# One weight block ahead of an activation tile, and a small early read of the other weight blocks

## The chip, the cores and the metric

The kernel runs on one core of a Trainium2 chip. TensorE (PE) multiplies, VectorE (DVE), ScalarE (ACT) and GpSimd (POOL) do the elementwise work, SyncE (SP) and ScalarE issue DMA transfers, which run on the core's 16 DMA engines. The metric is the device time of the whole program in microseconds (us).

## The reference

A linear-attention block and a dense GELU block share one layer-normalized input, and both are added to it:

```
xn = _layernorm(A_x)                       # A_x: 1 x 2048 x 640, bf16
# A: 32 heads of 20
q, k, v = split(xn @ wqkv)
phi(t) = where(t > 0, t + 1, exp(t)) + 1e-6
kv  = einsum("bhsd,bhse->bhde", phi(k), v);  z = einsum("bhsd->bhd", phi(k))
o   = einsum("bhqd,bhde->bhqe", phi(q), kv) / (einsum("bhqd,bhd->bhq", phi(q), z) + 1e-6)
A   = o @ wo
# B: F = 1536
B   = gelu(xn @ w1 + b1) @ w2 + b2
out = A_x + A + B
```

## The kernel before

Tokens are cut into 16 tiles of 128 (x0 to x15), the width 640 into 5 blocks of 128 (DT = 5), the hidden width 1536 into 12 blocks (JT = 12). W1 is loaded in five row blocks of 128 x 1536, one for each block of the contraction; each is 384 KB, a token tile of x is 160 KB.

The program issues every engine's instructions in the order in which they are written. A small planner (class Planner) notes for each tile who wrote it and who reads it, and gives an instruction the semaphore waits that follow; it doesn't reorder. Each DMA has a semaphore of its own, which sixteen increments complete.

The kernel has these stages: the hidden layer (xn @ w1, GELU) for all tokens while x, W1 and then the other weights arrive; the key features (L556 on); two products over tokens; the query features with the small products between; and the output, which sums over HG (the hidden layer) and PQ (the query features).

The change touches the first microseconds. SP issues, in order (L268 to L277): x0, x1, W1's row blocks 0 to 3 (`dma_w1`, L266), x2, W1's block 4, x3, and then x4 to x11 in three DMAs. ScalarE issues one early load, b1 (L449), after the warming activation at L448.

Meanwhile PE runs nine products on zeros (L318, L452; the last six open the accumulation in six banks). Tile 0 is normalized: statistics on DVE (`ln_half`, L331) with a small addition on POOL (L334), aggregation and reciprocal on DVE (L339, L342), a square root on ACT (L343), and three partial normalizations on DVE (`norm_part`, L398). PE transposes the pieces (`transp_part`, L404) and ACT copies them back (`copy_part`, L415). Tile 1 follows on the same engines, but takes its inverse root by a power on POOL (L346), and its first copy is on DVE (L413).

The hidden layer of tiles 0 and 1 is made block by block of the contraction, so that it can begin when W1's first block is there. `pass_k(k, t, n, ...)` (L421, matmuls at L424) multiplies W1's row block k for all twelve hidden blocks with n tiles from t on. PE's queue has, from the first of these on: pass 0 of tile 0 (four matmuls), the last transposes of tile 0, the other eight of pass 0, pass 1, **the five transposes of tile 1**, pass 2 of tile 0, the transpose of b1 (L323), passes 0 to 2 of tile 1, and passes 3 and 4 for both tiles at once, with the GELUs on ACT (L432). Tiles 2 and 3 follow (`h_two`, L439) and then wider units (`h_unit`, L380).

The buffer kT (two buffers of 128 x 512) is used by the key features: `phi` writes it (L562) and a DMA transposes it from there (L563). Nothing writes it before.

Of the kernel before, what the change touches and what calls it, by code (L numbers as in the profile page):

```python
# [7 lines left out]
P = 128  # L8
# [104 lines left out]
def bass_parallel_sum__linear_attn_block__dense_activation_gelu__prompt_kernel(  # L113
# [8 lines left out]
    DT = D // P  # L122
# [15 lines left out]
    with contextlib.ExitStack() as es:  # L138
# [41 lines left out]
        kT = sb("kT", [P, 2, CW], BF16)  # L180
# [55 lines left out]
        r_kT = [R_("kT%d" % i) for i in range(2)]  # L236
# [19 lines left out]
        def dma_x(t, n):  # L256
            src = xv[t * P:(t + n) * P, :].rearrange("(t p) d -> p t d", p=P)
            Pl.ins("sync", lambda e: e.dma_start(x_in[:, t:t + n, :], src),  # L258
                   writes=r_x[t:t + n], dma=True)

        def dma_w(eng, dst, src, res):
            Pl.ins(eng, lambda e: e.dma_start(dst, src), writes=[res], dma=True)

        w1v = B_w1.rearrange("(k p) n -> p k n", p=P)
        wqv = A_wqkv.rearrange("(k p) n -> p k n", p=P)
        def dma_w1(k):  # L266
            dma_w("sync", W1[:, k, :], w1v[:, k, :], r_W1[k])
        dma_x(0, 1)  # L268
        dma_x(1, 1)
        for k in range(4):  # L270
            dma_w1(k)
        dma_x(2, 1)
        dma_w1(4)
# [42 lines left out]
        def filler(n):  # L316
            b = take(1)
            Pl.ins("tensor", [lambda e: e.matmul(bank(b), warm[:, 0:P], warm[:], start=True, stop=True)  # L318
                              for _ in range(n)], reads=[r_warm], writes=[B_[b]])
# [126 lines left out]
                    reads=[B_[b], r_b1c], writes=[r_HG[t][jb + a]])  # L446

        Pl.ins("scalar", lambda e: e.activation(b1c[:, 0:1], warm[:, 0:1], ACT.Sqrt), reads=[r_warm], writes=[r_b1c])  # L448
        dma_w("scalar", b1tmp[:], B_b1.rearrange("(a p) -> a p", p=P), r_b1tmp)  # L449
        filler(3)  # L450
        for i in range(NB):
# [419 lines left out]
```

## Time and profile before

| | |
|---|---|
| median of 3 runs | 205.04 us (204.85 to 205.44) |
| the profiled execution | 204.63 us |
| its span (first to last instruction) | 203.2 us |
| PE busy | 198.3 us (98% of the span) |
| DVE, ACT, POOL busy | 122.2, 73.5, 13.7 us |
| granted TensorE clock | 1.0 |
| x0, x1, W1 block 0: issue to landing | 2.2, 2.2 and 4.4 us |

In the profile, rows of instructions have line, engine, operation, the tile written and the tile read, the shapes, a count, and the time. PEld is the weight load of TensorE. "Idle before" is the time that the engine waited just ahead, with what ended it in brackets. A W1 row block appears as "W" read from in_B_w_dram. The chain that ended last is followed back from the last instruction to what released each; its rows are start, length and what. Matmuls are pipelined, so a row's length runs to a modelled end, and neighbouring starts tell the pace.

### The profile page before, as it was taken

Reading aid. Unit: us, or ns where it says so; the run is one execution under the profiler, and the core shown is the slowest. Engines: PE = TensorE matmul, PEld = TensorE weight load, DVE = VectorE, ACT = ScalarE, POOL = GpSimd, SP = SyncE. Lnnn points to the kernel's source line nnn. Section 1 sums busy time; section 2 is a strip of 40 time slices with the busy share of each in tenths; the row PEclk is TensorE's granted clock in tenths of the full one; section 3 lists DMA queues with packets and bytes.
Section 4 is the critical chain, followed back from the end, with each engine's and each line's share of the span. In section 5 each row is a group of like instructions: output and inputs, shape, how many; then the busy total and the mean of one; then the engine's idle time right before and its main releaser. Section 6 shows DMA issues by size and latency. Waiting matters only on the chain.

```text
span 203.2 us, 3231 instructions
## 1 busy us (share of the span) xinstructions
PE 198.3 (98%) x1178; PEld 106.9 (53%) x1195; DVE 122.2 (60%) x246; ACT 73.5 (36%) x148; POOL 13.7 (7%) x41
## 2 busy tenths in 40 slices
PE   6899999999999999999999999999999999999996
PEld 2799984444444444644456565444444444444444
DVE  3669873000005899999458899693893685356222
ACT  3469996666667555111233596200000000000000
POOL 1135444000000000000000000000000000000000
DMA  6964898899901111000269935119276727633521
GB/s 164 391 224 97 135 203 112 269 320 267 277 0 26 26 26 29 0 0 0 41 185 374 147 65 105 48 36 161 39 104 198 147 45 150 165 76 64 168 77 52
DMA packets 51285, 25.45 MB, mean 125 GB/s; under 512 B 38134, under 2 KB 50630, under 8 KB 51270
## 3 DMA queue, kind: packets, MB, share of 16 engines
q1 hardware_dynamic: 47790, 24.07, 49.2%
q10 hardware_dynamic: 3480, 1.18, 2.5%
q8 instruction: 9, 0.15, 0.3%
q14 instruction: 6, 0.05, 0.1%
HBM read 12.72 MB, written 2.62 MB: 76 GB/s over the span
## 4 chain that ended last, share of the span: by engine, by line
PE 96%; DMA 2%; issue 1%; SPq 0%; DVE 0%
PE ps L780 29%; PE ps L380 19%; PE ps L619 11%; PE ps L608 8%; PE ps L567 8%; PE ps L745 7%; PE ps L424 3%; PE ps L439 3%; DMA W<-in_B_w_dram 2%; PE ps L598 2%; PE ps L558 2%; PE ps L633 1%; PE ps L651 1%; SPq L258 0%; PE ps L404 0%
## 5 line engine op out<-in xcount | busy, mean ns | idle before, releaser
L780 PE MATMUL ps<-HG,W 128*128 128x512 bf16 x188 | 41.9, 379 | 0.2
L380 PE MATMUL ps<-xnT,W 128*128 128x512 bf16 (+1 forms) x222 | 39.0, 336 | 0.2
L380 PEld LDWEIGHTS ps<-xnT,W 128*128 128x128 bf16 x225 | 22.0, 98 | 16.7
L780 PEld LDWEIGHTS ps<-HG,W 128*128 128x128 bf16 x192 | 18.8, 98 | 22.6
L384 ACT ACTIVATE HG<-ps,b1c 128x512 bf16<-128x512 f32 (+1 forms) x45 | 26.3, 667 | 11.3 <-PE ps L380 10.8
L619 PE MATMUL ps<-xnT,Wqkv 128*128 128x512 bf16 x97 | 22.4, 380 | 0.2
L567 PE MATMUL ps<-Wqkv,xnT 128*128 128x512 bf16 x78 | 17.8, 379 | 0.1
L780 PE MATMUL ps<-PQ,Msb 128*128 128x512 bf16 x78 | 17.8, 379 | 0.1
L608 PE MATMUL ps<-xPK,xn_tm 128*128 128x512 bf16 x78 | 17.2, 379 | 0.1
L331 DVE BATCH_NORM_STATS2 stats<-xPK 128x6 f32<-128x320 bf16 x32 | 13.8, 470 | 4.3 <-DMA xPK<-in_A_x_dram 4.3
L619 PEld LDWEIGHTS ps<-xnT,Wqkv 128*128 128x128 bf16 x100 | 11.3, 118 | 8.7
L542 ACT ACTIVATE xn_tm<-ps 128x512 bf16<-128x512 f32 x20 | 11.9, 597 | 9.5 <-PE ps L619 8.9
L786 DVE SCALAR_TENSOR_TENSOR W<-ps,b2c,xnT 128x512 bf16<-128x512 f32 x16 | 11.6, 738 | 5.9 <-PE ps L780 5.5
L545 DVE SCALAR_TENSOR_TENSOR PQ<-ps,xn_tm 128x512 bf16<-128x512 f32 x20 | 13.8, 692 | 2.1
L542 ACT ACTIVATE ek<-ps 128x512 bf16<-128x512 f32 x20 | 11.8, 597 | 8.4 <-PE ps L567 6.4
L553 DVE CAST b2c<-out_l 128x5 f32<-128x5 bf16 x1 | 0.2, 172 | 22.4 <-DMA out_l<-b2bc 22.4
L567 PEld LDWEIGHTS ps<-Wqkv,xnT 128*128 128x128 bf16 x80 | 7.8, 98 | 9.4
L780 PEld LDWEIGHTS ps<-PQ,Msb 128*128 128x128 bf16 x80 | 7.8, 98 | 9.4
L608 PEld LDWEIGHTS ps<-xPK,xn_tm 128*128 128x128 bf16 x80 | 7.8, 98 | 9.3
L668 DVE SCALAR_TENSOR_TENSOR xn_tm<-PQ,z_sb,xn_tm 128x512 f32<-128x512 bf16 x16 | 12.0, 750 | 0.4
L684 DVE TENSOR_REDUCE den_sb<-xn_tm 128x128 f32<-128x512 f32 x4 | 4.2, 1040 | 13.4 <-DMA xn_tm<-xn_tm 13.4
L545 DVE SCALAR_TENSOR_TENSOR xPK<-ps,ek 128x512 bf16<-128x512 f32 x16 | 11.1, 692 | 1.7
(73 smaller groups left out, 182.2 us busy)
## 6 DMA issues: line engine op xcount, KB each, us to landing
xPK<-in_A_x_dram SPq DMA_DIRECT2D x5, 640.0 KB, 8.1
Wqkv<-in_A_wqkv_dram SPq DMA_DIRECT2D x3, 800.0 KB, 6.8
W<-in_B_w_dram SPq DMA_DIRECT2D x5, 384.0 KB, 5.4
W<-in_B_w_dram SPq DMA_DIRECT2D x1, 1920.0 KB, 14.8
out_dram<-xPK SPq DMA_DIRECT2D x3, 640.0 KB, 3.5
xPK<-in_A_x_dram SPq DMA_DIRECT2D x4, 320.0 KB, 5.3
xn_tm<-xn_tm ACTq DMA_DIRECT2D x12, 64.0 KB, 3.2
Wo<-in_A_wo_dram SPq DMA_DIRECT2D x1, 750.0 KB, 11.5
```

Of the source, the lines that this page charges most:

```text
L331: Pl.ins(v, lambda e: e.bn_stats(stats[:, s, 6 * h:6 * h + 6], x_in[:, t, h * HW:(h + 1) * HW]), reads=[r_x[t]], writes=[r_stats[s][h]])
L380: Pl.ins("tensor", [(lambda e, k=k: e.matmul(bank(b, 0, w), W1[:, k, jb * P:(jb + 1) * P], xnT[:, k, tok], start=(k == 0), stop=(k == DT - ...
L384: Pl.ins("scalar", lambda e: e.activation(HG[:, jb, tok], bank(b, 0, w), ACT.Gelu_apprx_tanh, bias=b1c[:, jb:jb + 1]), reads=[B_[b], r_b1c ...
L542: Pl.ins("scalar", lambda e: e.activation(et, src, ACT.Exp), reads=[B_[b]], writes=[re])
L545: Pl.ins(v, lambda e: e.scalar_tensor_tensor(out=dst, in0=src, scalar=0.0, in1=et, op0=ALU.max, op1=ALU.add), reads=[B_[b], re], writes=[r ...
L567: Pl.ins("tensor", [(lambda e, k=k, b=b, t=t: e.matmul(bank(b), xnT[:, k, t * P:(t + 1) * P], Wqkv[:, k, D:D + CW], start=(k == 0), stop=( ...
L608: Pl.ins("tensor", lambda e, t=t, b=b, f=f: e.matmul(bank(b), xn_tm[:, t, f * P:(f + 1) * P], PK[:, t, 0:CW], start=(t == 0), stop=(t == N ...
L619: Pl.ins("tensor", [(lambda e, k=k, j=j, b=b: e.matmul(bank(b), Wqkv[:, k, j:D:DT], xnT[:, k, cc], start=(k == 0), stop=(k == DT - 1))) fo ...
L668: Pl.ins(v, lambda e: e.scalar_tensor_tensor(out=yv[c % 2], in0=pq, scalar=z_sb[:, j:j + 1], in1=yv[c % 2], op0=ALU.mult, op1=ALU.add), re ...
L745: return lambda e: e.matmul(bank(b, 0, cs.stop - cs.start), l, r[:, cs], start=(i == 0), stop=(i == JT + DT - 1))
L780: Pl.ins("tensor", lambda e, l=l, r=r, i=i: e.matmul(bank(b), l, r, start=(i == 0), stop=(i == JT + DT - 1)), reads=rd, writes=[B_[b]], ma ...
L786: Pl.ins(v, lambda e: e.scalar_tensor_tensor(out=oT[o], in0=bank(b), scalar=b2c[:, nb:nb + 1], in1=xnT[:, nb, cc], op0=ALU.add, op1=ALU.ad ...
```

## The change

SP now issues x0, W1's block 0, x1, and then W1's blocks 1 to 3; the rest keeps its order. ScalarE issues one more DMA ahead of b1's: it reads 32 elements (64 bytes) of the first 16 rows of each of W1's row blocks 1 to 4 and writes them into the first buffer of kT, on 16 partitions. What it writes is never read; the planner registers it as a writer of that buffer. Nothing else is different (line numbers after it move by one or two).

```diff
@@ -266,8 +266,9 @@
         def dma_w1(k):
             dma_w("sync", W1[:, k, :], w1v[:, k, :], r_W1[k])
         dma_x(0, 1)
+        dma_w1(0)
         dma_x(1, 1)
-        for k in range(4):
+        for k in range(1, 4):
             dma_w1(k)
         dma_x(2, 1)
         dma_w1(4)
@@ -446,6 +447,7 @@
                     reads=[B_[b], r_b1c], writes=[r_HG[t][jb + a]])
 
         Pl.ins("scalar", lambda e: e.activation(b1c[:, 0:1], warm[:, 0:1], ACT.Sqrt), reads=[r_warm], writes=[r_b1c])
+        dma_w("scalar", kT[0:16, 0, 0:P].rearrange("p (k n) -> p k n", k=4), w1v[0:16, 1:DT, 0:32], r_kT[0])
         dma_w("scalar", b1tmp[:], B_b1.rearrange("(a p) -> a p", p=P), r_b1tmp)
         filler(3)
         for i in range(NB):
```

## The prediction

> **What bounds the kernel now.** I read the busy shares first. PE is busy for nearly the whole span, at full granted clock, so time can only be won or lost where PE waits.
>
> ```profile
> span 203.2 us, 3231 instructions
> PE 198.3 (98%) x1178; PEld 106.9 (53%) x1195; DVE 122.2 (60%) x246; ACT 73.5 (36%) x148; POOL 13.7 (7%) x41
> ```
>
> Then the chain that ended last, in order of time, for the first 16 us. The reader is to see that it enters PE at 6.17 through the load of W1's first row block, and that from 8.40 on it is PE work with no wait.
>
> ```profile
> 1.73 4.40 DMA W<-in_B_w_dram
> 6.13 0.05 issue
> 6.17 0.40 PE ps L424 x4
> 6.57 0.11 PE ps L404 x2
> 6.68 0.45 PE ps L424 x8
> 7.13 0.02 issue
> 7.15 0.84 PE ps L424 x12
> 8.00 0.41 PE ps L404 x5
> 8.40 0.67 PE ps L424 x12
> ```
>
> This chain would promise up to half a microsecond: the first product of pass 0 also needs a copy (L415) that ends at 5.59, so with W1's block 0 there PE could start near 5.65 instead of 6.17. But the five transposes at 8.00 (L404, token tile 1) stand in PE's queue ahead of pass 2, and they wait for something else. So third I read VectorE's timeline.
>
> ```profile
> 4.68 0.82 DVE L398 TENSOR_SCALAR xn_tm<-xPK,aggr,rstd 128x128 bf16<-128x128 bf16 x3 [0.27 <-ACT rstd L343]
> 5.42 0.88 DVE L331 BATCH_NORM_STATS2 stats<-xPK 128x6 f32<-128x320 bf16 x2
> 6.40 0.21 DVE L339 BATCH_NORM_AGGREGATE aggr<-stats 128x2 f32<-128x12 f32 x1
> 7.37 0.64 DVE L398 TENSOR_SCALAR xn_tm<-xPK,aggr,rstd 128x256 bf16<-128x256 bf16 x2 [0.76 <-POOL rstd L346]
> ```
>
> The statistics of x1 start at 5.42 with no idle time ahead of them: DVE has just finished tile 0. Statistics, aggregation, GpSimd's power (6.69 to 7.26) and the two normalizations follow without a gap that anything else fills. The second normalization ends at 8.00, and the single matmul records show the third transpose starting at 8.06. The two before it start at 7.83 and 7.89; at the 0.056 us between neighbours the third would have come at 7.94 had it waited for W1 alone. So at 8.06 two chains meet, the W1 side ready at 7.94 and the x1 side at 8.06, and **the x1 side already ends last**. From the start of x1's statistics to that transpose are 8.06 - 5.42 = 2.64 us.
>
> Last, the landings. A DMA counts sixteen engines and is complete with the last. Asked issue by issue, the DMA view gives 2.2 us from issue to landing for x0 and for x1, and 4.4 for W1's block 0. In the trace's records of the increments x0 is complete at 2.98, x1 at 3.58, block 0 at 6.13, block 1 at 7.11, block 2 at 8.05. Block 0's sixteen increments are thirteen from 4.84 to 5.07, then 5.22, 5.69 and 6.13. Why so late shows in the stretches of the DMA traffic (columns: stretch, length, busy of PE, PEld, DVE, ACT, POOL, clock, DMA share, GB/s):
>
> ```profile
> 2.80:3.20 0.40, 0.40 (x2) 0.15 (x1) 0.20 (x1) 0.00 (x0) 0.00 (x0) 1.00 1.48 360
> 3.20:3.60 0.40, 0.40 (x2) 0.15 (x1) 0.40 (x2) 0.00 (x0) 0.02 (x1) 1.00 0.82 92
> 3.60:4.00 0.40, 0.40 (x2) 0.15 (x1) 0.29 (x2) 0.00 (x0) 0.21 (x1) 1.00 0.67 200
> 4.00:4.80 0.80, 0.77 (x3) 0.10 (x1) 0.49 (x3) 0.20 (x1) 0.00 (x0) 1.00 1.08 346
> ```
>
> From 3.2 to 4.0 the engines move little. In the packet records a W1 packet (3072 B) takes 0.121 us, but the first ones of block 0 take 0.35 to 0.84, and one, at 3.91, takes 1.14. Block 1's first packets, at 4.4 to 4.7, take 0.12 to 0.62; x packets (1280 B) take 0.055, the first ones of x0 and x1 up to 0.39. [...] the slowest engine carries it along: it stays some 0.45 us behind the second slowest from block 0 to block 3.
>
> [...] b1's packets, ScalarE's one early load, lie at 2.30 to 2.79 among x0's and x1's. [...]
>
> **The change part by part.**
>
> (1) W1's block 0 is issued before x1. SP's issues are 0.47 apart (0.80, 1.27, 1.73), so block 0 is issued at 1.27 and x1 at 1.73; all later SP issues keep place and time, and the engines have a backlog anyway. Per engine block 0 is 8 packets, 8 x 0.121 = 0.97 us, and x1 is 8 x 0.055 = 0.44. Block 0 no longer has x1's 0.44 ahead of it: it is complete near 6.13 - 0.44 = 5.7, and PE starts at about 5.7, 0.45 earlier. Pass 1 still waits for block 1, which has the same bytes ahead as before (7.11), so the W1 side stays at 7.94. This saves nothing at 8.06.
>
> x1 now is the last of the first three transfers. The bytes of x0, x1 and block 0 together are what they were, so if the stalls stay, x1 is complete when block 0 was: 6.13. VectorE is free for it at 5.42. The statistics start at 6.13 + 0.03 = 6.16, 0.74 later, and all behind them on DVE (aggregation, normalization, the copy L413) and POOL shift likewise; the third transpose starts at 6.16 + 2.64 = 8.80. PE, done with pass 1 near 7.9, idles. Pass 2 is late by 0.74, and so is everything after, since from 8.40 on the chain has no other wait that could absorb it (x2, 9.43, has about 1 us of slack in front of it on DVE). Cost: +0.74. If x1's engines are all as quick as the fifteenth was (5.69) it is 5.72 - 5.42 = +0.30; if as the thirteenth (5.07), nothing. So x1 costs nothing when complete by 5.39 and one for one after that.
>
> (2) The small read: one more DMA issue on ScalarE ahead of b1's. The only such row is b1's issue, 0.63 us from 1.23; now the small one takes 1.23 to 1.86 and b1's follows to about 2.5. ScalarE's next work that matters is the square root at 4.44: hidden by 1.9 us; b1 itself is first used by a transpose at 9.0. The transfer is 64 packets of 64 bytes, four per engine, one in each block 1 to 4, arriving near 2.30 as b1's packets did. Moving them costs little: b1's 256 B packets took 0.018 us, so 4 x 0.018 = 0.07 per engine. What they may cost is first-read stalls, in front of block 0 and x1, and for engines not yet through with x0 (its packets run to about 2.6) in front of x0. The trace shows no such read. Below: none, as the stalls run beside the one that block 0's first packet has anyway (0.23 to 0.72 over the 0.121); an early read of W1 could even shorten block 0's long second stall (1.14 - 0.12 = 1.0), a gain for x1 of up to 0.74, after which DVE binds. Above: four stalls in a row of block 1's worst excess, 0.62 - 0.12 = 0.50 each, 2.0 us. I take 0: mostly beside block 0's own stall, with some delay against some relief. The stalls of blocks 1 to 4 that go away save nothing, as x1 binds.
>
> (3) The scratch is kT's first buffer, whose first true write is by DVE in the key phase, after 60 us: one more wait, long met. Nothing.
>
> Sum: 0 for W1 + 0.74 for x1 + 0 for the small read = +0.74, on the profiled execution 204.63 + 0.74 = 205.37 (span 203.2 + 0.74 = 203.9, and 1.4 around it as before). The profiled execution lies 0.41 below the median of the runs shown, 205.04; on that median it is 205.78, so 205.8.
>
> **The rivals.** Bounds first: I call 0.3% (0.62 us), about what a measurement of this kernel can tell from no change, the edge of "same".
>
> Rival A, not slower: x1 is complete by about 5.4 to 5.9 because the long stall doesn't come back, cured by the small read or mere bad luck of one engine. For it: thirteen of sixteen engines were done with block 0 by 5.07, and x1 would need only those. It decides at x1 complete at 5.39, and up to 5.39 + 0.62 = 6.01 it stays within "same". Time 205.0 to 205.6. Against: the last engine decides[...].
>
> Rival B, much slower: the small read's stalls come one after the other, or in front of x0's last packets, where each delays tile 0 as well and so everything one for one. +0.74 plus 0.5 to 2.0: 206.3 to 207.8. For it: b1's packets reach the engines at 2.30, when x0 isn't through. Against: x packets follow each other at 0.055 us although a whole DMA takes 2.2 from issue to landing, so reads overlap within an engine, and four stalls can too.
>
> Rival C, faster: W1's blocks stall longer in the timed runs than in the profiled one (the 0.41), and the small read removes that, while x1 comes in time. Then PE gains what it waits for W1 beyond 8.06: at most some 0.4 to 0.8, 204.2 to 204.6. Against: nothing of it shows in the profile, where the x1 side ends last.
>
> **How the numbers follow.** Forecast (x1 late by 0.6 to 1.2): 0.42; rival A 0.37; B 0.14; C 0.07. Forecast and B are slower by over 0.3%: 0.56. A is "same": 0.37. C is faster: 0.07. The predicted time is the forecast's, 205.8, its own range 205.6 to 206.3. The range for 8 in 10 leaves out most of C and the far end of B: 204.7 to 206.8.
>
> **What would show it.** Right: block 0 complete at 5.6 to 5.8 and PE's first L424 there; DVE's second pair of L331 with an idle time in front put down to x's DMA, starting at about 6.1; PE idle ahead of the tile 1 transposes, which end near 9.1 instead of 8.40; and the same shift, not more, at each later point of the chain. Wrong: if the second pair of L331 still starts at 5.42, the forecast falls for A; if the first pair starts after 3.00, the small read sits in front of x0 (B); if the chain's 8.40 comes earlier, then tile 1's transposes weren't bound by x1 as I read them.

## The result, and the profile after

The changed kernel took 206.77 us (median of 4 runs, 206.36 to 206.98), the kernel before 205.24 us beside it (204.85 to 205.45, 4 runs): a ratio of 1.0074, 95% interval 1.0051 to 1.0098. Later sets of the same two kernels, below, do not repeat that ratio. Of the later runs 18 were over 1.5% above the fastest of their kernel (17 of the kernel before, one of the small read alone) and are left out of the counts, group medians and means below.

The page of the kernel after, its span and busy time:

```profile
span 205.3 us, 3249 instructions
PE 199.6 (97%) x1195; PEld 106.9 (52%) x1195; DVE 122.5 (60%) x246; ACT 74.5 (36%) x148; POOL 13.7 (7%) x41
```

The span is 2.1 us longer. The chain that ended last (start, length, what) now enters PE through x1, not through W1:

```profile
1.73 4.10 DMA xPK<-in_A_x_dram
5.83 0.02 issue
5.85 0.90 DVE stats L332 x2
...
7.81 0.36 DVE xn_tm L399
8.16 0.05 issue
8.21 0.29 PE ps L405 x2
8.50 0.00 issue
8.50 0.34 PE ps L405 x3
8.84 0.67 PE ps L425 x12
```

x1 is complete at 5.83, its statistics start at 5.85 instead of 5.42, and pass 2 starts 0.44 later (8.84 for 8.40). PE's own timeline shows both sides of the swap: the first product starts 0.38 earlier than before (5.79 for 6.17) and waits for ACT's copy, no longer for W1, whose block 0 is complete at 4.77 instead of 6.13; and PE idles 0.54 ahead of tile 1's transposes, where it didn't before.

```profile
5.79 0.38 PE L425 MATMUL ps<-xnT,W 128*128 128x128 bf16 x4 [0.15 <-ACT xnT L416]
8.21 0.63 PE L405 MATMUL ps<-ident,xn_tm 128*128 128x128 bf16 x5 [0.54 <-DVE xn_tm L399]
```

So far this is the forecast with 0.44 in place of 0.74. Comparing the two traces weight load by weight load, the changed kernel is 0.43 late from tile 1's transposes on, and 2.07 late from the first weight load of L380 (L381 after the change) on, until the end. The second loss, 1.64, is one wait. The chain of the kernel before from 14 us on goes from tiles 2 and 3 (L439) to the wider units (L380) without a wait:

```profile
14.20 6.88 PE ps L439 x120
21.07 8.95 PE ps L380 x82
```

The chain of the kernel after between 14 and 30 us:

```profile
14.63 6.88 PE ps L440 x120
21.52 1.44 issue
22.96 7.15 PE ps L381 x64
```

At 21.52 PE has finished tiles 2 and 3 and stands until 22.96. "Issue" means that the profile names nothing that it waited for; what it needs there is tiles 4 and 5, whose transposes are DMAs (L506). In the DMA view of the issue of tile 5's transpose (count, time from issue to landing) the kernel after has

```profile
xnT<-xn_tm SPq DMA_TRANSPOSE x1, 4.3
```

against, in the kernel before,

```profile
xnT<-xn_tm SPq DMA_TRANSPOSE x1, 2.6
```

where it was issued at 18.09 and complete at 20.66, 0.19 ahead of PE's need at 20.85. In the kernel after it was issued at 18.52 and complete at 22.87. The DMA queues of the kernel after from 20.4 to 21.8 (queue, packets, MB, time as a share of 16 engines):

```profile
q1 hardware_dynamic: 456, 0.11, 122.9%
q8 instruction: 1, 0.02, 5.1%
```

The packet of the second row is a 16 KB fetch of instructions, at 20.50, 1.14 us long; in these two traces such fetches (0.88 to 1.41 us) recur every 78 to 164 weight loads of PE, counted at their ends. Here it begins as the transpose's last packets are due. In the kernel before the fetch of that place began at 21.78, after tile 5 and within tile 6's transpose, which then took 4.3 us (19.41 to 23.71) and was not yet needed.

### The profile page after: what moved, and what is told of

Read it like the earlier page. It is cut to its first block, busy times and chain, and to the rows that moved or that the text cites. A ratio compares the mean times of both kernels' runs of the same rounds, so it can differ in the third digit from the quotient of the medians.

```text
span 205.3 us, 3249 instructions
## 1 busy us (share of the span) xinstructions
PE 199.6 (97%) x1195; PEld 106.9 (52%) x1195; DVE 122.5 (60%) x246; ACT 74.5 (36%) x148; POOL 13.7 (7%) x41
## 4 chain that ended last, share of the span: by engine, by line
PE 94%; DMA 2%; issue 1%; DVE 1%; SPq 0%; POOL 0%; DVEq 0%
PE ps L782 29%; PE ps L381 19%; PE ps L621 11%; PE ps L569 8%; PE ps L610 8%; PE ps L747 7%; PE ps L440 3%; PE ps L425 3%; PE ps L600 2%; PE ps L560 2%; DMA xPK<-in_A_x_dram 2%; PE ps L635 1%; PE ps L653 1%; DVE stats L332 0%; PE ps L405 0%
## 5 line engine op out<-in xcount | busy, mean ns | idle before, releaser
L381 PE MATMUL ps<-xnT,W 128*128 128x512 bf16 (+1 forms) x225 | 39.1, 336 | 1.4 <-issue 1.4
L385 ACT ACTIVATE HG<-ps,b1c 128x512 bf16<-128x512 f32 (+1 forms) x45 | 27.1, 605 | 12.0 <-PE ps L381 10.8
L381 PEld LDWEIGHTS ps<-xnT,W 128*128 128x128 bf16 x225 | 21.9, 98 | 18.3 <-issue 1.6
L547 DVE SCALAR_TENSOR_TENSOR xPK<-ps,ek 128x512 bf16<-128x512 f32 x16 | 11.1, 692 | 1.7
L588 DVE TENSOR_TENSOR Msb<-Msb,xPK 128x640 f32<-128x640 f32 x14 | 11.6, 825 | 0.5
```

The source lines that it names most:

```text
L381: Pl.ins("tensor", [(lambda e, k=k: e.matmul(bank(b, 0, w), W1[:, k, jb * P:(jb + 1) * P], xnT[:, k, tok], start=(k == 0), stop=(k == DT - ...
L385: Pl.ins("scalar", lambda e: e.activation(HG[:, jb, tok], bank(b, 0, w), ACT.Gelu_apprx_tanh, bias=b1c[:, jb:jb + 1]), reads=[B_[b], r_b1c ...
L547: Pl.ins(v, lambda e: e.scalar_tensor_tensor(out=dst, in0=src, scalar=0.0, in1=et, op0=ALU.max, op1=ALU.add), reads=[B_[b], re], writes=[r ...
```

## The experiments

Two theories stood at first. Theory L: x1's lateness does it all, the second wait included. Rival R: x1's lateness costs only its own part, and the small read does the rest, by its stalls or by its additional instruction. All edits are to one of the two kernels shown above. The times of every kernel fall in two groups, and I split them at 205.95 us:

| kernel | runs | below: count, median | above: count, median |
|---|---|---|---|
| before, four sets beside the others | 195 | 124, 204.91 | 71, 206.57 |
| changed, first set | 4 | 0 | 4, 206.77 |
| changed, two later sets | 28 | 20, 205.15 | 8, 206.33 |
| order of the loads alone | 22 | 11, 205.45 | 11, 207.03 |
| small read alone | 13 | 9, 205.00 | 4, 206.77 |
| x1's statistics made late on DVE | 22 | 14, 205.29 | 8, 206.99 |
| before, ten products more | 22 | 7, 204.96 | 15, 206.59 |
| before, re-cut, two sets | 44 | 41, 205.00 | 3, 206.63 |
| changed, re-cut | 22 | 21, 205.13 | 1, 205.97 |
| order alone, re-cut | 22 | 22, 205.53 | 0 |
| small read alone, re-cut | 22 | 20, 204.98 | 2, 206.40 |
| changed with the read from W2, re-cut | 22 | 21, 205.29 | 1, 207.00 |

**The order of the loads alone.** The changed kernel without the small read:

```diff
-        dma_w("scalar", kT[0:16, 0, 0:P].rearrange("p (k n) -> p k n", k=4), w1v[0:16, 1:DT, 0:32], r_kT[0])
```

> The order of the loads alone (x0, W1 block 0, x1, the other blocks), without the small read. The profile of the change shows two losses: x1 complete at 5.83 instead of 3.58, which moves tile 1's transposes by 0.43 us, and a wait of 1.4 us of PE at 21.5 for tile 5's DMA transpose, during which a 16 KB instruction fetch stood on a DMA engine. Theory L (lateness alone): both losses come from x1 being late, the small read does nothing; this kernel loses 1.3 to 1.7 us as the whole change does, and the profile shows PE's wait before L380 again. Rival R (the small read): the order of the loads costs only x1's 0.3 to 0.7 us, and PE doesn't wait near 21; the rest belongs to the small read or to its additional instruction.

Measured: 205.86, 1.0033 of before (1.0006 to 1.006), in two groups of eleven. Its profiled execution is of the upper group, and PE waits 1.55 near 22 there. So the second wait needs no small read, and R falls. But x1 is not the only late load: in this profile block 1 of W1 is complete at 8.14 (7.11 before), and pass 1 waits for it.

**The small read alone.** The changed kernel with the loads in their old order:

```diff
         dma_x(0, 1)
-        dma_w1(0)
         dma_x(1, 1)
-        for k in range(1, 4):
+        for k in range(4):
             dma_w1(k)
```

> The small read alone, with the loads in their old order. Theory L: x1 is complete near 3.6 to 4.2, DVE's statistics of tile 1 start near 5.4, no loss, within 0.3 us of the kernel before. Rival R: a loss of 0.8 us or more, with PE waiting near 21 for a DMA transpose or with first-read stalls ahead of x0 or x1. If the small read shortens W1's stalls, block 0's and block 1's landings come before 6.13 and 7.11.

Measured: 205.24, ratio 1.0000 (0.9968 to 1.0032), x1 complete at 3.65. The read costs nothing that shows. Nor does it take W1's stalls away: its 64 packets took at most 0.011 us each, without a stall of their own, and in the same profile the longest W1 packet took 1.41 us (1.14 in the profile of before).

**Lateness alone.** The kernel before with a memset on DVE ahead of x1's statistics:

```diff
         turn_0(1)
+        Pl.ins(v, lambda e: e.memset(ek[:, 0:2, 0:420], 0.0), writes=r_ek[0:2])
         ln_stats(1)
```

> The kernel before with nothing moved among the DMAs; one memset of about 0.44 us on VectorE ahead of x1's statistics makes tile 1 as late as in the change. Theory L: tile 1's transposes are 0.4 us later and, if the lateness alone brings on the second wait, the loss is 1.5 to 2 us with PE waiting before L380 near 21. Rival R: the loss is the 0.4 us alone.

Measured: the statistics start at 6.00, 0.58 later than before; the profiled execution is 0.51 late from tile 1's transposes to the end, with no second wait, and the lower group stands at 205.29, 0.38 above before's. The upper group's share is 8 of 22, before's 71 of 195. So lateness passes to the end nearly one for one and doesn't bring on the second wait: theory L falls in its second half.

**The changed kernel again.** No edit.

> The changed kernel once more, beside the others on the same chip. Both theories: 1.3 to 1.8 us slower than before. If the second wait is a matter of chance in each execution, the profile may lack it and the times spread over 0.4 to 2 us of loss; if it belongs to the program, PE waits 1.2 to 1.6 us before L381 near 21.5 again.

> The changed kernel a third time. The first four runs of it all stood near 206.7, of the next fourteen eleven stood near 205.2 and three near 206.3. If the first four were chance, the two groups here are again shared as in the kernel before (about 60 to 40) and the lower one is 0.2 to 0.3 us above before's lower one; if the change makes the wait for tile 5's transpose likelier, the upper group holds clearly more than before's 40%.

Measured: 0.9995 of before (0.9967 to 1.0022) and 1.0006 (0.9972 to 1.0040). Of the 28 runs 8 are in the upper group. The two later profiles part as the groups do: in the first PE passes 21.2 without a wait, in the second (span 204.9) it waits 1.3 there and tile 5's transpose took 4.15 us. The first set, all four runs of the changed kernel in the upper group and all four of before in the lower, is not what they do in the later sets. At before's share such a split would come in 0.3% of cases (0.364 to the fourth, times 0.636 to the fourth), so chance alone is a poor account of it, and what was different there is open.

**The need for tile 5 put off.** If the upper group is the wait for tile 5's transpose, it goes when tile 5 is needed later. PE takes tiles 4 and 5 one after the other for eight hidden blocks:

```diff
-        units(4, 2, 0, 9)
+        for t in (4, 5):
+            for jb in range(0, 8, 2):
+                h_two(t, jb)
+        units(4, 2, 8, 9)
         units(6, 2, 0, 9)
```

> The kernel before, with PE's work after tiles 2 and 3 re-cut: tiles 4 and 5 are first taken one at a time for eight hidden blocks (80 products of 128 columns for 40 of 256), tile 5 after tile 4, so that tile 5's DMA transpose is needed about 2.3 us later. The times of every kernel so far fall in two groups 1.6 us apart, near 205.0 and near 206.6. Theory F (a 16 KB instruction fetch of PE falls on one DMA engine during tile 5's transpose, PE waits for it): the upper group disappears, all runs within 204.8 to 205.5, the re-cut costs 0 to 0.3 us. Rival: the upper group has another cause and about 40% of the runs still stand near 206.6.

> The re-cut kernel without the change once more, as the version that should beat both kernels. Theory F: all but one or two of its runs near 205.0, as before (21 of 22), while the kernel before has some 40% of its runs near 206.6: about 0.3% faster on the mean, with the interval below 1. If the first set was chance, a group near 206.6 appears here too.

Measured: in the two sets 3 of 44 runs are above 205.95, and over all kernels with this edit 7 of 132; the kernel before without it has 71 of 195. The lower group pays 0.09 for it (205.00 for 204.91). Each set gives a ratio of 0.9984, intervals 0.9966 to 1.0002 and 0.9962 to 1.0007; the means over all runs are 205.17 (standard error 0.07) and 205.55 (0.06). Each interval alone just includes no change; the means are 0.4 us apart.

With the profiles this shows that the upper group is the wait for tile 5: PE waits 1.26 to 1.67 us ahead of tiles 4 and 5 in all four profiled executions of the upper group without this edit, and not at all in the four of the lower group. Why the edit removes it is less sure. In all six profiles with the edit tile 5's transpose took 2.57 at most, so none of them shows a late transpose that PE no longer waits for; the edit may also have moved the fetches, and six profiles are too few to tell. The three remaining runs above 205.95 need not have this cause, and one was caught by the profile of the second set (span 205.4). Its PE timeline:

```profile
6.64 0.61 PE L424 MATMUL ps<-xnT,W 128*128 128x128 bf16 x4 [0.82 <-DMA W<-in_B_w_dram]
7.04 0.42 PE L404 MATMUL ps<-ident,xn_tm 128*128 128x128 bf16 x2
7.25 2.34 PE L424 MATMUL ps<-xnT,W 128*128 128x128 bf16 x20
```

and the same rows of the first set (span 203.4):

```profile
5.89 0.38 PE L424 MATMUL ps<-xnT,W 128*128 128x128 bf16 x4 [0.19 <-ACT xnT L415]
6.11 0.28 PE L404 MATMUL ps<-ident,xn_tm 128*128 128x128 bf16 x2
6.23 1.28 PE L424 MATMUL ps<-xnT,W 128*128 128x128 bf16 x20
```

Twenty matmuls take 2.34 us for 1.28. Block 0 came late (6.60), PE stood 0.82, and then ran at about half pace until 11.1 (neighbouring matmuls start 0.107 us apart for 0.056). The clock column of this profile reads 1.00 throughout, so the granted clock doesn't account for the half pace; what does is not shown, and it is one execution.

**The parts without the second wait.** The same edit on the changed kernel and on its two halves:

> The changed kernel with the same re-cut. Theory F with lateness of x1: one group, later than the re-cut kernel without the change by what x1's lateness costs, 0.1 to 0.5 us. If the change costs 1.5 us of its own, it shows here too.

> The order of the loads alone, re-cut. Lateness of x1 alone: +0.3 to +0.7 us against the re-cut kernel without it, spread by the length of the first-read stalls. If the small read helps, this one is slower than the whole change, re-cut, by 0.1 to 0.4; if it hurts, faster.

> The small read alone, re-cut. Expected +0.0 to +0.2 us: x0 completes up to 0.2 later with the small read's packets among its own, and W1's blocks are waited for a little less. A gain would mean that W1's stalls bound the kernel before in its timed runs.

Against the re-cut kernel before, of its two sets together (205.00): the whole change +0.13, the order alone +0.53, the small read alone -0.02. On the means of the lower groups (standard errors near 0.05) the first two are +0.11 and +0.38. So the order costs 0.4 to 0.5 us, and the small read, which does nothing alone, gives most of it back. Where the order's loss lies changes from execution to execution. Order alone, chain of its profile:

```profile
2.19 5.88 DMA W<-in_B_w_dram
8.07 0.05 issue
8.12 0.84 PE ps L425 x12
```

That is block 1, complete at 8.07, with x1 long there (5.34). In the profile of the whole change, re-cut, x1 is complete at 5.07 and costs nothing, and PE waits for block 2:

```profile
2.67 5.97 DMA W<-in_B_w_dram
8.64 0.05 issue
8.69 0.84 PE ps L425 x12
```

**The read from elsewhere.** The re-cut changed kernel, the small read from W2's rows:

```diff
-... w1v[0:16, 1:DT, 0:32], r_kT[0])
+... B_w2.rearrange("(k p) n -> p k n", p=P)[0:16, 1:DT, 0:32], r_kT[0])
```

> The whole change re-cut, with the small read taken from W2's rows instead of W1's. The re-cut order of the loads alone stood at 205.53, with the small read of W1 at 205.13. If the small read helps by touching W1 ahead of its blocks, this one is back near 205.5; if it helps by something else (its packets or its issue), near 205.1.

Measured: 205.29, between 205.13 and 205.53. The means of the three lower groups are 205.35, 205.17 and 205.43, with standard errors of 0.04 to 0.06: the read from W2 is clearly slower than the read from W1, and not clearly faster than no read. It doesn't tell the two explanations apart.

**Ten products more.** The kernel before, with ten small products more on PE, to move the fetches by ten weight loads:

```diff
         filler(3)
+        Pl.ins("tensor", [lambda e: e.matmul(bank(7, 0, 64), warm[:, 0:P], warm[:, 0:64], start=True, stop=True)
+                          for _ in range(10)], reads=[r_warm], writes=[B_[7]])
```

> The kernel before, with ten small products on zeros (64 columns) added while PE waits for x0. They shift PE's instruction fetches by ten weight loads, some 0.6 us earlier against tile 5's transpose, and cost nothing else. Theory F (fetch against transpose decides the group): the fetch near 21 comes 0.5 us earlier and the share near 206.6 changes clearly from 40%, up to 70 to 100% if it now mostly falls into tile 5's transpose. Rival: the share stays near 40%.

Measured: the upper group rises to 15 of 22; at a share of 71 in 195 so many or more come in 0.2% of cases. That speaks for the instruction fetch. The lower group stays at 204.96, so the products themselves cost nothing. In the four profiled executions with the wait at 21 (the changed kernel's first and third, the order alone, this one) the fetch began 1.87 to 2.53 us after tile 5's transpose was issued and the transpose took 4.15 to 4.56; in the other ten it began 2.30 to 3.69 after and the transpose took 2.57 at most. The two ranges overlap between 2.30 and 2.53. In two of the four slow transposes (the order alone, this one) fifteen of the sixteen increments came on time, 2.4 to 2.6 us after the issue, and the last one 1.9 to 2.0 us later, as if one DMA engine alone was held up; in the other two all sixteen came late. No run took the fetch itself away: that the fetch holds the transpose up is well supported, not shown.

## Why the prediction was right or wrong

**The direction held, and so did the path through x1.** "The x1 side already ends last" is confirmed by the late statistics on DVE: tile 1's transposes are 0.51 later in its profile, and so is the end, while W1's blocks 0 to 2 came only 0.19 to 0.24 later than before. In the first profile of the change the wait for x1 (5.83) stands in the chain where it was forecast.

**The term for x1 was too large.** I put x1's completion at 6.13 by letting every stall of the kernel before recur. It was 5.83, 5.46 and 5.07 in the changed kernel's three profiles, and the statistics start 0.43, 0.10 and 0.14 later. x0 itself was 0.05, 0.10 and 0.14 later, so x1's own term, forecast at 0.74, was about 0.4 in the first profile and nothing in the other two. The forecast's x1, late by 0.6 to 1.2, is in none of them; rival A, x1 complete by about 5.4 to 5.9, describes all three. The two later sets have their lower group at 205.15, 0.24 above before's, within A's 205.0 to 205.6.

**"Complete near 6.13 - 0.44 = 5.7" failed, without a cost.** Block 0 was complete at 4.77, 4.70 and 4.63: the long stall that had held it until 6.13 did not recur in it. In the first profile PE's start (5.79) then waited for ACT's copy, the bound that the prediction had put near 5.65.

**"The W1 side stays at 7.94" failed.** The bytes ahead of blocks 1 and 2 are unchanged, but the stalls are not: block 1 was complete at 8.14 and 8.07 with the order alone, block 2 at 8.41 to 8.64 in three of four profiles of the change, against 7.11 and 8.05. By the re-cut runs the order's cost is 0.4 to 0.5 in all, and part of it may lie here, a term that I had set to nothing. But the old order varies as much: over its seven profiles block 1 was complete at 6.49 to 8.07 and block 2 at 7.42 to 9.02. I had read one execution's stalls as the kernel's, and how much of the later landings is due to the order is not shown.

**"From 8.40 on the chain has no other wait that could absorb it" failed in the other direction.** The chain had no wait, but it passed 20.85 with 0.19 to spare: tile 5's transpose was complete at 20.66. I looked for slack that would swallow a delay and not for a transfer that was only just in time. The 1.64 that followed in the profile is the larger part of the recorded loss. It is not the change's: the kernel before has it in 71 of 195 runs, the changed one in 8 of 28 of the later sets.

**The small read.** "I take 0" holds for its own cost, and its ScalarE issue took 0.41, less than the 0.63 I took. Rival B, its stalls in a row, didn't come: no packet of it took over 0.011. Its relief, which I weighed at nothing, is 0.4 on the medians beside the new order (205.53 to 205.13), 0.26 on the means, and how it works is open; W1's packets still stall up to 1.69 us with it.

**Rival C** named the timed runs as slower than the profiled one. They are, in two groups, but not through W1, and the change didn't remove it.

So the recorded 206.77 is the profiled 204.63 with 0.43 and 1.64 added (206.70); the forecast of 205.8 had the first term too large and the second not at all. That 206.77 lies within the stated 204.7 to 206.8 is luck: most of the excess is a wait that the prediction did not have and that the change did not make. Over the later sets the change's own cost is 0.1 to 0.25 us, within what I called the same.

## What to carry to other kernels

When a chain shows no wait at all, list the transfers that end just ahead of it and by how much: a slack of 0.19 us on a DMA is a bound in waiting, and over a third of the executions of this kernel pay for it. Before a difference of 1.5 us is explained, run the unchanged kernel often enough to see whether its own times fall in groups; here four runs of each didn't. A load moved behind another is costed by the last of its sixteen increments (that of W1's block 0 came 1.06 us after the thirteenth in the profile of before), and the stalls that decide it do not stay where one profile showed them (block 1 complete at 6.49 to 8.07 over seven profiles of the old order): take several profiles of the unchanged kernel before a landing time goes into a sum.

## What the runs showed of the hardware

An instruction fetch of 16 KB is one packet of 0.9 to 1.8 us in the fourteen profiles, on one DMA engine by the view above (1.14 us in 1.4 us of sixteen engines are its 5.1%). I take these fetches for PE's: a run has nine, ten where PE was given 40 products more, 78 to 169 weight loads apart, and from the fourth on they start within one weight load of the same place in the first profiles of both kernels. Tile 5's transpose by DMA took 4.2 to 4.6 us for 2.6 in four of the fourteen profiles, each time with such a fetch beginning before its normal end; in four of the others a fetch began before that end too, without delaying it. Tile 6's transpose, issued 1.3 us later, took 4.3 to 5.1 in all fourteen. In the trace the kernel's transfers (q1) and the fetches (q8) are separate queues. That a fetch on one engine makes the single late increments above (1.9 to 2.0 us late) is my reading; how an engine serves the two queues is not shown.

Packets of W1 (0.121 us as a rule) can stall: the longest took 0.6 to 1.9 us in each of the fourteen profiles, with or without an earlier read of the same blocks. Beyond 0.121 us a packet, W1's packets took 0.56 to 1.21 us more for each engine, on the mean of the sixteen. The early read, of 64 bytes in 16 of the 128 rows of each block, did not end these stalls; that they belong to the first read of a region, as the prediction had it, is not shown.
